# Rows of attention stored unscaled beside their norms; weight conversion from head pair 1

## The chip, the cores and the metric

One core of one Trainium2 chip runs the whole program in one launch. The metric is device time in microseconds (us). A core has a matrix engine (PE, with its weight loads PEld), a vector engine (DVE), an activation engine (ACT), GpSimd (POOL) and a sync engine (SP); each runs its own instructions in order, and they meet through semaphores. Here SP and POOL issue the DMAs: SP the plain loads, POOL the indirect ones and the stores of x.

## The reference, cut to what matters

```
kv  = k^T v per batch and head           # 8 x 8 heads, 576 x 64
o   = q kv ; x = o / rms(o) * g_norm     # rms over the 64 columns of a head
logits = x @ w_gate                      # 4608 tokens, 8 experts
# greedy assignment in order of falling logits, 576 tokens for each expert
for e in experts: y[mask_e] = relu(x[mask_e] @ w1[e]) @ w2[e]
h = y @ w_in ; out = (h * cos(h)) @ w_out
```

x has 4608 rows of 512 columns (8 heads of 64). Each head of each row has one norm factor, 1/rms; g_norm is folded into w1 and w_gate.

## The kernel before

**Attention.** Batches go two at a time (four stages s), heads two at a time, so 16 head pairs n. For each, PE builds k^T v, transposes q and multiplies; ACT copies the result into `xs` (stage 1 uses the room of `wout`) and squares it, DVE sums the squares into `SS` and copies q and k^T v to SBUF. At the end of a stage `norm(s)` queues small steps on DVE that give the factors `R`; then POOL multiplies x by R in place, head pair by head pair (`scaled`, four instructions a stage), and stores the stage's 2304 KB to `x_rows` in HBM. The gate's logits are scaled by DVE with the same factors.

**Routing.** `Router.phase(k)` finds expert k's tokens: DVE compares keys, PE counts, eight rounds. Phase 0 stands between attention and the rest; phases 1 to 7 are worked in among later matmuls. `widx` (which weights) is known some us before `idx` (which tokens).

**Experts.** Tokens go in 16 blocks of 288 (`u`). `h`, `y`, `h2`, `outs` are the matmul stages of a block. POOL gathers the rows of x by `idx`, five tiles of up to 128 rows for an expert; `xtile` transposes a tile on PE, and ACT and DVE copy it out as two f16 halves. w1 and w2 of an expert are gathered by POOL; each is squared for a scale and split into a high half (ACT) and a low half (DVE).

**Conversion of the dense weights.** w_in and w_out come as 32 units of 512 KB in 64-bit words (`dense`). A unit is loaded by SP into one of three `io` buffers, scaled by ACT (`dG`) and merged by three DVE instructions into `stA` or `stB`. Four units make a block: two sums of squares on ACT, then for each of two tiles a high half on ACT and a low half on DVE (`win`, `wout`). All of w_in has to be done before `h2` of block 0, all of w_out (`("out", 3)`) before the first `outs`.

**What sets the order.** A planner (`Meter`, `Sched`) keeps a modelled clock for each engine while the program is written out. Pieces of the conversion are put between other work where they end no later than the modelled PE clock plus a slack (`PA` in attention). `GRANT` says after which head pair how many more units may be loaded. In attention the conversion starts after pair 4 (`n > 4`). `Sched.FILL` is the order in which kinds of fill are tried. `first_load` issues w1 and w2 of expert 0: all of w1 and the first two tiles of w2 as soon as `widx` is known, the other two once the second w1 tile is split and the gather of x is issued.

Of the kernel before, what the change touches and what calls it, by code (L numbers as in the profile page):

```python
# [8 lines left out]
F32 = mybir.dt.float32  # L9
# [4 lines left out]
OP = mybir.AluOpType  # L14
# [2 lines left out]

B, H, S, D = 8, 8, 576, 64
N, DM = B * S, H * D
E = 8  # L20
NCOL = 36


def dview(t, off, ap):
    return bass.AP(tensor=t.tensor, offset=t.offset + off, ap=ap)


PA = (3.6, 3.5, 33.0, 2.48, 2)
RB = 9
LOADED = 13  # L30
GRANT = {5: 1, 7: 1, 9: 1, 11: 1, 12: 2, 13: 99}
NHP = H // 2


def attention(nc, tc, q, k, v, w_gate, xrows, ident, gcol, L, M, sc):


    with ExitStack() as st:
# [27 lines left out]
        W2 = 2 * (D + E)  # L66
        KV = [one.tile([128, 2, NHP, W2], F32, name=f"KV{i}") for i in range(2)]
        SS = one.tile([128, NCOL, H], F32, name="SS")
        R = one.tile([128, NCOL, H], F32, name="R")
        kvt, qTs, XS, LR = {}, {}, {}, {}  # L70
        late, held = [], []
        M.prf = lambda: ps.tile([128, 4, 128], F32, name="pT", bufs=2).rearrange("p a b -> p (a b)")
# [73 lines left out]
        def o_mm(n, g):  # L146
            s, hp = divmod(n, NHP)
            if hp == 0 and g == 0:
                if s == 1:
                    XS[s] = M.wout2.rearrange("p i f d -> p (i f d)").bitcast(F32)[:, 0:RB * H * D].rearrange(  # L150
                        "p (r h e) -> p r h e", r=RB, h=H)
                else:
                    XS[s] = wk.tile([128, RB, H, D], F32, name="xs", bufs=2)
                LR[s] = wk.tile([128, RB, H, E], F32, name="LR", bufs=2)
            qT, kv = qTs.pop((n, g)), kv_of(n)
            pO = ps.tile([128, 2, 512], F32, name="pO", bufs=2)
            J, N = (1, 1) if g == 2 else (2, 2)
            for j in range(J):
                for a in range(2):
                    o = (D + E) * (2 * j + a)  # L160
                    for X in range(2):
                        for i in range(N):
                            h = slice(64 * i, 64 * i + 64)
                            nc.tensor.matmul(pO[64 * X:64 * X + 64, i, o:o + D + E],
                                             qT[h, 2 * j + X, 64 * a:64 * a + 64],
                                             kv[h, X, (D + E) * a:(D + E) * a + D + E], start=True, stop=True)
            hs = slice(2 * hp, 2 * hp + 2)
            if g < 2:
                po = pO[:, :, 0:2 * W2].rearrange("p i (j e) -> p j i e", j=2)
                rows = lambda x: x[:, 4 * g:4 * g + 4, hs].rearrange("p (j i) a e -> p j i (a e)", i=2)  # L170
                srows = lambda x: x[:, 4 * g:4 * g + 4, hs]
                lrows = lambda x: x[:, 4 * g:4 * g + 4, hs].rearrange("p (j i) a e -> p j i a e", i=2)
            else:
                po = pO[:, 0, 0:W2]
                rows = lambda x: x[:, 8, hs].rearrange("p a e -> p (a e)")
                srows = lrows = lambda x: x[:, 8, hs]
            sq = wk.tile([128, 4, 2, D], F32, name="sq", bufs=2)
            sqv = sq[:, 0].rearrange("p a e -> p (a e)") if g == 2 else sq.rearrange("p (j i) a e -> p j i (a e)", i=2)
            nc.scalar.activation(sqv, po[..., E:E + 2 * D], AF.Square)
            nc.scalar.activation(rows(XS[s]), po[..., E:E + 2 * D], AF.Copy)  # L180
            later()
            nc.vector.tensor_copy(lrows(LR[s]), gates(po))
            nc.vector.tensor_reduce(srows(SS[:, RB * s:RB * s + RB]), sq[:, 0] if g == 2 else sq, axis=AX, op=OP.add)
            later()
            if g == 2 and hp == NHP - 1:
                norm(s)

        def norm(s):
            c = slice(RB * s, RB * s + RB)
            a, y, w = (wk.tile([128, RB, H], F32, name=nm, bufs=1) for nm in ("na", "ny", "nw"))  # L190
            x = XS[s]
            m = LR[s]

            def scaled(i):
                h = slice(2 * i, 2 * i + 2)
                nc.gpsimd.tensor_mul(x[:, :, h], x[:, :, h], R[:, c, h, None].to_broadcast([128, RB, 2, D]))

            def store():
                nc.gpsimd.dma_start(dview(xrows, 2 * s * S * DM, [[RB * DM, 128], [1, RB * DM]]),
                                    x.rearrange("p r h e -> p (r h e)"))  # L200

            def stored():
                if s in HOLD:
                    held.append(store)
                else:
                    store()

            late.extend([
                lambda: nc.vector.tensor_scalar(a, SS[:, c], 1.0 / D, 1e-6, op0=OP.mult, op1=OP.add),
                lambda: nc.scalar.activation(w, a, AF.Sqrt),  # L210
                lambda: nc.vector.reciprocal(y, w),
                lambda: nc.vector.scalar_tensor_tensor(w, y, -0.5, y, op0=OP.mult, op1=OP.mult),
                lambda: nc.vector.tensor_mul(w, w, a),
                lambda: nc.vector.scalar_tensor_tensor(R[:, c], w, 1.5, y, op0=OP.add, op1=OP.mult),
                lambda: nc.vector.tensor_mul(m, m, R[:, c, :, None].to_broadcast([128, RB, H, E])),
                lambda: nc.vector.tensor_reduce(L[:, c, :], m.rearrange("p r h e -> p r e h"), axis=AX, op=OP.add),
            ] + [lambda i=i: scaled(i) for i in range(NHP)] + [stored])

        def side():
            later()  # L220
# [5 lines left out]
        for n in range(NP + 1):  # L226
            steps = []
            if n < NP:
                steps.append(lambda: kv_mm(n))
            if n:  # L230
                steps += [lambda: (o_mm(n - 1, 0), tr(n - 1, 2))]
            if n < NP:
                steps.append(lambda: kw_t(n))
            if n:
                steps.append(lambda: o_mm(n - 1, 1))
            if n < NP:
                steps.append(lambda: (tr(n, 0), kw_mm(n)))
            if n:
                steps.append(lambda: o_mm(n - 1, 2))
            if n < NP:  # L240
                steps.append(lambda: tr(n, 1))
            M.grant += GRANT.get(n, 0)
            for f in steps:
                f()
                if n == LOADED:
                    while held:
                        held.pop(0)()
                    HOLD.clear()
                if n > 4:
                    side()  # L250
                else:
                    later()
# [458 lines left out]
class Sched:  # L711
# [3 lines left out]

    FIRST = ("w0", "x0")
    FILL = ("w0", "x0", "l0", "bt", "bd", "bg", "p")

    def __init__(self, meter):
        self.m = meter
# [153 lines left out]
class Moe:  # L876
# [252 lines left out]
    def first_load(self, which, room, alloc):  # L1129
        sc, js = self.sc, (range(2), range(2, 4))  # L1130
        while 0 not in self.R.widx:
            yield WAIT
        for i in range(2):
            if i:
                for mark in room:
                    yield from sc.until(mark)
            for j in js[i]:
                yield "gpsimd", 1.04, self.R.known
                self.load_w(which, 0, [j], alloc[i])
                self.land[which, j] = self.nc.last  # L1140
# [42 lines left out]
    def gather(self, k, js=range(5)):  # L1183
        cb = 9 * k // 2
        for j in js:
            n = 64 if j == 4 and k % 2 == 0 else 128
            if k:
                t = self.pers.tile([128, 1024], F32, name="io", bufs=3)[:, 0:DM]
            else:
                t = self.tmp.tile([128, 2, U], F32, name=("et", "et", "eg", "eg", "ek")[j], bufs=1 + (j < 4))  # L1190
                t = t.rearrange("p a b -> p (a b)")[:, 0:DM]
            self.nc.gpsimd.indirect_dma_start(
                out=t[0:n], out_offset=None, in_=self.xrows,
                in_offset=bass.IndirectOffsetOnAxis(ap=self.R.idx[0:n, cb + j:cb + j + 1], axis=0))
            self.xg[k, j] = t, self.nc.last

    def xtrans(self, k, js=range(5), pre={}):
        for j in js:
            if j in pre:
                self.gather(k, [pre[j]])  # L1200
            yield from self.sc.after(self.xg[k, j][1])
            self.xtile(k, j)
            yield "both"

    def first_x(self, js):
        for j in js:
            yield "tensor", 0.45, self.xg[0, j][1]
            self.xtile(0, j)

    def xtile(self, k, j):  # L1210
        nc = self.nc
        r0, r1 = (64, 128) if k % 2 and j == 0 else (0, 64) if k % 2 == 0 and j == 4 else (0, 128)
        n = r1 - r0
        pos = 128 * j - 64 * (k % 2 and j > 0)
        x = self.xg[k, j][0]
# [203 lines left out]

def body(ctx, tc, q, k, v, g_norm, w_gate, w1, w2, w_in, w_out, out):  # L1420
    nc = Meter(tc.nc)
    xrows = nc.dram_tensor("x_rows", (N, DM), F32, kind="Internal").ap()
    ctx.enter_context(tc.manual_schedule())
    pers = ctx.enter_context(tc.tile_pool(name="pers", bufs=1))
    sm = ctx.enter_context(tc.tile_pool(name="sm", bufs=2))
# [49 lines left out]
    M.far = True  # L1475
    for n in range(E):
        sc.add("route", R.phase(n), ("route", n))
    sc.add("l0", M.first_load(1, (), [istage, istage]))
    sc.add("l0", M.first_load(2, (("w1", 0, 1), "gx"), [istage, istage]))
    sc.add("w0", M.first_w(1), ("w1", 0))  # L1480
    sc.add("w0", M.first_w(2), ("w2", 0))
    GP = (0.39, 1.67, 38.72, 0.83)
# [105 lines left out]
```

## Time and profile before

| | us |
|---|---|
| median of 3 runs (1458.42 to 1464.58) | 1463.87 |
| the profiled execution | 1462.46 |
| its span, first to last instruction | 1460.7 |
| PE / DVE / ACT / POOL busy in the span | 1334.3 / 890.4 / 617.8 / 190.7 |
| attention; routing phase 0 (to `idx`) | 0 to 150; 150 to 195 |
| first blocks, w_out conversion ends the wait | 195 to 323 |

The profiled execution lies 1.41 us under the median. The page's forty slices show PE at 9 tenths or more from the tenth slice on, and at 2 to 8 in the nine before. Nearly every compute instruction is recorded at one helper's line (L689), so instructions are told apart by the tiles that they write and read.

### The profile page before, as it was taken

To read this page: it belongs to the slowest core of one execution; us is meant where nothing else is said; L and a number is where in the kernel's file an instruction comes from. 1 tells how busy PE (TensorE), PEld (TensorE's weight loads), DVE (VectorE), ACT (ScalarE), POOL (GpSimd) and SP (SyncE) were. 2 spreads that over 40 slices of the span, in tenths; PEclk is the share of its full clock that TensorE was granted. 3 is DMA by queue.
4 is the path that set the end of the run, shared out by engine and by line. 5 is a ranking of instruction groups with operands and counts; after the bars stand their busy time and mean duration, and the time that the engine had idled before them with its cause. 6 is when DMAs were issued, how large, how long until landed. Compare 5 with 4: busy or idle time off the path is not lost.

```text
span 1460.7 us, 28545 instructions
## 1 busy us (share of the span) xinstructions
PE 1334.3 (91%) x12072; PEld 910.9 (62%) x12072; DVE 890.4 (61%) x2096; ACT 617.8 (42%) x1031; POOL 190.7 (13%) x211
## 2 busy tenths in 40 slices
PE   5877248859999999999999999999999999999997
PEld 4656235636667574666667675867676667676663
DVE  2658888887858676586667673655365426544350
ACT  2546255744625341446134621653256225533240
POOL 0222240003011111022002100130022001000000
PEclk8886559979999999999999999999999999999999
DMA  7795353213111111032002200140013002000000
GB/s 276 268 340 226 123 180 113 70 62 123 51 66 42 65 31 65 9 95 73 1 16 91 73 2 22 34 133 2 15 60 104 1 22 71 18 1 15 8 8 22
DMA packets 40367, 109.32 MB, mean 75 GB/s; under 512 B 4272, under 2 KB 12464, under 8 KB 39728
## 3 DMA queue, kind: packets, MB, share of 16 engines
q0 software_dynamic: 15744, 62.40, 12.5%
q1 hardware_dynamic: 23808, 45.09, 8.9%
q8 instruction: 94, 1.54, 0.4%
q14 instruction: 33, 0.27, 0.1%
q10 hardware_dynamic: 688, 0.02, 0.0%
HBM read 88.62 MB, written 18.87 MB: 74 GB/s over the span
## 4 chain that ended last, share of the span: by engine, by line
PE 77%; DVE 4%; ACT 2%; DMA 1%; issue 1%; POOL 0%; POOLq 0%; ACTq 0%; DVEq 0%; SPq 0%
PE ph L689 74%; PE pr L689 3%; PE pq L689 1%; DVE eg L689 1%; DVE stB L689 0%; ACT junk L689 0%; DMA sti<-in_moe_w_dram,wi 0%; DVE yT L689 0%; DMA io<-in_moe_w_out_dram 0%; DMA stB<-in_moe_w_dram,wi 0%; ACT ek L689 0%; DVE gT L689 0%; DVE stA L689 0%; ACT wout L689 0%; DVE wout L689 0%
## 5 line engine op out<-in xcount | busy, mean ns | idle before, releaser
L689 PE MATMUL ph<-wout,gT 128*128 128x512 f16 x1728 | 390.2, 380 | 5.0 <-DVE eg L689 2.6
L689 PE MATMUL ph<-yT,win 128*128 128x288 f16 x3072 | 384.2, 286 | 0.9 <-DVE eg L689 0.8
L689 PEld LDWEIGHTS <-win 128*128 128x128 f16 x3072 | 297.6, 98 | 78.9 <-DVE eg L689 1.8
L689 PEld LDWEIGHTS <-gT 128*128 128x128 f16 x1728 | 162.6, 98 | 202.4 <-ACT junk L689 11.1
L689 ACT ACTIVATE ek<-ph,quarter,us 128x576 int32<-128x576 f32 x128 | 106.3, 830 | 327.1 <-PE ph L689 320.1
L689 PE MATMUL ph<-xT,w1s 128*128 128x288 f16 x1536 | 202.7, 291 | 9.3 <-DVE hT L689 6.4
L689 PE MATMUL ph<-hT,w2s 128*128 128x288 f16 x1536 | 202.7, 286 | 0.0
L689 DVE SCALAR_TENSOR_TENSOR et<-ph,us,ek 128x576 f32<-128x576 f32 x128 | 104.6, 817 | 135.5 <-ACT ek L689 135.2
L689 PEld LDWEIGHTS <-w1s 128*128 128x128 f16 x1536 | 149.5, 99 | 50.8 <-DVE hT L689 3.7
L689 PEld LDWEIGHTS <-w2s 128*128 128x128 f16 x1536 | 146.2, 98 | 36.3
L689 POOL DMA_INDIRECT out_dram<-eg,idx x36 | 36.7, 1021 | 606.6 <-DVE scT L689 299.5
L689 DVE SCALAR_TENSOR_TENSOR eg<-ph,cG,et 128x576 f32<-128x576 f32 x128 | 103.5, 809 | 2.7 <-ACT et L689 1.3
L689 DVE TENSOR_TENSOR gT<-eg,gT 128x576 f16<-128x576 f32 (+2 forms) x192 | 99.6, 550 | 0.7
L689 ACT ACTIVATE gT<-eg 128x576 f16<-128x576 f32 (+2 forms) x192 | 92.3, 513 | 14.9 <-DVE eg L689 14.9
L689 ACT ACTIVATE et<-et,qtr 128x576 f32<-128x576 f32 x128 | 97.9, 765 | 0.6 <-DVE et L689 0.6
L689 DVE TENSOR_TENSOR eg<-ph,scT 128x512 f32<-128x512 f32 x36 | 24.9, 692 | 112.9 <-PE ph L689 109.0
L689 ACT ACTIVATE yT<-ph,sy 128x576 f16<-128x576 f32 x32 | 22.0, 737 | 163.1 <-DVE sy L689 156.8
L689 DVE SCALAR_TENSOR_TENSOR hT<-ph,hT 128x576 f16<-128x576 f32 x64 | 48.0, 755 | 50.0 <-ACT hT L689 49.7
L689 ACT ACTIVATE hT<-ph 128x576 f16<-128x576 f32 x64 | 40.9, 646 | 82.4 <-PE ph L689 82.4
L689 POOL DMA_INDIRECT io<-x_rows,idx x35 | 34.2, 978 | 240.7 <-PE pq L689 198.5
L689 POOL DMA_INDIRECT stA<-in_moe_w_dram,wi x28 | 29.8, 1063 | 225.0 <-issue 187.8
L689 PE MATMUL pO<-KV,qTs 64*64 64x72 f32 x1152 | 41.0, 264 | 12.5 <-issue 9.9
(209 smaller groups left out, 1328.7 us busy)
## 6 DMA issues: line engine op xcount, KB each, us to landing
kt<-in_k_dram SPq DMA_DIRECT2D x16, 576.0 KB, 5.2
vt<-in_v_dram SPq DMA_DIRECT2D x16, 576.0 KB, 6.6
qt<-in_q_dram SPq DMA_DIRECT2D x16, 576.0 KB, 7.4
io<-in_moe_w_in_dram SPq DMA_DIRECT2D x16, 512.0 KB, 6.6
io<-in_moe_w_out_dram SPq DMA_DIRECT2D x16, 512.0 KB, 3.5
x_rows<-xs POOLq DMA_DIRECT2D x3, 2304.0 KB
x_rows<-wout POOLq DMA_DIRECT2D x1, 2304.0 KB
out_dram<-eg,idx POOLq DMA_INDIRECT x36
```

The lines of the kernel that those rows point to most:

```text
L689: return f(*a, **kw)
```

## The change

`R` is gone. A row of x is now 520 values: 512 unscaled columns and the 8 factors, written by DVE into the last 8 columns of `xs`; rows of `x_rows` are 2080 bytes. POOL's sixteen multiplications are gone, and the stage's store is queued right behind the logits. The factor is applied after the gather: `xnorm`, one DVE instruction a tile (40 tiles, five an expert), ahead of the tile's transposes. Conversion may be placed from head pair 1 on, one unit granted for each pair, with other slacks. w2's first two tiles are loaded after the gather of x. x is tried before w0 in `FILL` and `FIRST`.

```diff
-PA = (3.6, 3.5, 33.0, 2.48, 2)
+PA = (2, 2, 33.0, 2.48, 2)
-GRANT = {5: 1, 7: 1, 9: 1, 11: 1, 12: 2, 13: 99}
+GRANT = {**dict.fromkeys(range(1, 13), 1), 13: 99}
...
-            def scaled(i):
-                h = slice(2 * i, 2 * i + 2)
-                nc.gpsimd.tensor_mul(x[:, :, h], x[:, :, h], R[:, c, h, None].to_broadcast([128, RB, 2, D]))
...
-                lambda: nc.vector.scalar_tensor_tensor(R[:, c], w, 1.5, y, op0=OP.add, op1=OP.mult),
+                lambda: nc.vector.scalar_tensor_tensor(r, w, 1.5, y, op0=OP.add, op1=OP.mult),
...
-            ] + [lambda i=i: scaled(i) for i in range(NHP)] + [stored])
+                stored,
+            ])
...
-                if n > 4:
+                if n:
                     side()
...
-    FIRST = ("w0", "x0")
-    FILL = ("w0", "x0", "l0", "bt", "bd", "bg", "p")
+    FIRST = ("x0", "w0")
+    FILL = ("x0", "w0", "l0", "bt", "bd", "bg", "p")
...
     def xtrans(self, k, js=range(5), pre={}):
-        for j in js:
+        for j in (*js, None):
+            if j is not None:
+                yield from self.sc.after(self.xg[k, j][1])
+                self.xnorm(k, j)
+            if j != js[0]:
+                self.xtile(k, js[-1] if j is None else j - 1)
...
+    def xnorm(self, k, j):
+        r0, r1 = self.xspan(k, j)
+        x = self.xg[k, j][0][r0:r1]
+        y = x[:, 0:DM].rearrange("p (h e) -> p h e", h=H)
+        self.nc.vector.tensor_mul(y, y, x[:, DM:XW, None].to_broadcast([r1 - r0, H, D]))
...
-    sc.add("l0", M.first_load(1, (), [istage, istage]))
-    sc.add("l0", M.first_load(2, (("w1", 0, 1), "gx"), [istage, istage]))
+    sc.add("l0", M.first_load(1, ((), ()), [istage, istage]))
+    sc.add("l0", M.first_load(2, (("gx",), (("w1", 0, 1),)), [istage, istage]))
```

On POOL, at the end of attention and the gather for expert 0 (`sti` are the tiles of w1 and then w2; `et`, `eg`, `ek` the tiles of x), before:

```order
L689 TENSOR_TENSOR xs<-xs,R 128x9x128 x4
L689 DMA x_rows<-xs 128x4608
L689 DMA sti<-in_moe_w_dram,wi 128x1024 x6
L689 DMA et<-x_rows,idx 128x512 x2
L689 DMA eg<-x_rows,idx 128x512 x2
L689 DMA ek<-x_rows,idx 64x512
L689 DMA sti<-in_moe_w_dram,wi 128x1024 x2
```

The same place on POOL now:

```order
L687 DMA x_rows<-wout 128x4680
L687 DMA x_rows<-xs 128x4680 x2
L687 DMA sti<-in_moe_w_dram,wi 128x1024 x4
L687 DMA et<-x_rows,idx 128x520 x2
L687 DMA eg<-x_rows,idx 128x520 x2
L687 DMA ek<-x_rows,idx 64x520
L687 DMA sti<-in_moe_w_dram,wi 128x1024 x4
```

The multiplications are gone, and two tiles of w2 stand behind the gather instead of ahead of it.

On DVE, where expert 0's x is turned into `xT` and w1 is split (`peb` to `sg` is w1's scale), before:

```order
L689 TENSOR_SCALAR peb<-pq 128x1
L689 TENSOR_SCALAR s_3020<-peb 128x1
L689 TENSOR_TENSOR sg<-s_3020,gcol 128x1
L689 TENSOR_SCALAR stB<-dG 128x512
L689 SCALAR_TENSOR_TENSOR stB<-dG,stB 128x512
L689 TENSOR_TENSOR xT_2429<-ph,xT_2428 128x4x128 x3
L689 TENSOR_TENSOR xT_2429<-pq,xT_2428 128x4x128
L689 TENSOR_TENSOR xT_2429<-pq,xT_2428 128x4x64
L689 SCALAR_TENSOR_TENSOR w1s_2425<-sti,sg,w1s_2424 128x1024
```

The same place on DVE now:

```order
L687 TENSOR_SCALAR peb<-pq 128x1
L687 TENSOR_SCALAR s_3066<-peb 128x1
L687 TENSOR_TENSOR sg<-s_3066,gcol 128x1
L687 TENSOR_TENSOR et<-et 128x512
L687 SCALAR_TENSOR_TENSOR w1s_2456<-sti,sg,w1s_2455 128x1024
L687 TENSOR_TENSOR et<-et 128x512
L687 TENSOR_TENSOR xT_2460<-ph,xT_2459 128x4x128
L687 TENSOR_TENSOR eg<-eg 128x512
L687 TENSOR_TENSOR xT_2460<-ph,xT_2459 128x4x128 x2
L687 TENSOR_TENSOR eg<-eg 128x512
L687 SCALAR_TENSOR_TENSOR w1s_2456<-sti,sg,w1s_2455 128x1024
```

The factors' multiplications (`et<-et`, `eg<-eg`) stand between, the first low half of w1 comes ahead of the transposed tiles, and the merges have left this place.

On DVE, behind the last product (`eg`) of block 0's `h2`, before:

```order
L689 TENSOR_TENSOR gT_3313<-eg,gT_3312 128x2x288 x2
L689 TENSOR_SCALAR g_4109<-pr 15x8
L689 SCALAR_TENSOR_TENSOR stA<-io,stA 128x512
L689 TENSOR_SCALAR stA<-dG 128x512
L689 SCALAR_TENSOR_TENSOR stA<-dG,stA 128x512
L689 SCALAR_TENSOR_TENSOR stA<-io,stA 128x512
L689 TENSOR_REDUCE amy<-ph 128x1
```

The same place on DVE now:

```order
L687 TENSOR_TENSOR gT_3346<-eg,gT_3345 128x2x288 x2
L687 SCALAR_TENSOR_TENSOR stB<-dG,stB 128x512
L687 TENSOR_REDUCE nS<-pr 128x1
L687 TENSOR_TENSOR base<-base,nS 128x1
L687 SCALAR_TENSOR_TENSOR cmp<-hi,base,i_73 128x540
L687 TENSOR_REDUCE amy<-ph 128x1
L687 SCALAR_TENSOR_TENSOR stB<-io,stB 128x512
```

Of the 32 merges, 25 stood ahead of this place and 29 do now; of w_out's eight low halves two stood ahead of it and four do now. Ahead of routing phase 0 stood 7 merges and 2 low halves of w_in, and now 11 and 4; by the time that phase 0 has written `idx` it was 11 and 2, and is now 16 and 4.

## Rows read from the trace of the kernel before

**Rows 1.** Busy time by stage; the columns stand in its first line.

```profile
core 0: us, PE busy (x) PEld busy (x) DVE busy (x) ACT busy (x) POOL busy (x), PEclk, DMA share, GB/s
0.00:150.00 150.00, 107.59 (x2721) 86.93 (x2721) 87.15 (x230) 74.96 (x188) 31.15 (x30) 0.82 0.76 274
150.00:195.00 45.00, 12.07 (x336) 10.55 (x337) 38.69 (x108) 9.01 (x15) 16.61 (x11) 0.51 0.40 138
195.00:305.00 110.00, 88.52 (x696) 64.28 (x696) 94.19 (x197) 70.29 (x104) 9.43 (x7) 0.89 0.34 111
305.00:321.00 16.00, 0.45 (x3) 0.31 (x3) 12.82 (x29) 9.57 (x15) 0.00 (x0) 0.59 0.19 64
321.00:1460.70 1139.70, 1125.65 (x8317) 748.79 (x8315) 657.54 (x1535) 453.93 (x714) 133.53 (x163) 1.00 0.13 43
```

**Rows 2.** Timeline of PE: start, us, instruction, idle before and releaser.

```profile
319.10 0.16 PE L689 MATMUL pq<-psb,ones 128*128 128x1 bf16 x1 [10.83 <-DVE psb L689]
```

**Rows 3.** Timeline of DVE at the start of phase 0, then of phase 1.

```profile
151.55 0.76 DVE L689 TENSOR_TENSOR LR<-LR,R 128x576 f32<-128x576 f32 x1
...
154.53 2.10 DVE L689 TENSOR_SCALAR key<-m 128x36 int32<-128x36 int32 x1
...
156.92 2.11 DVE L689 TENSOR_TENSOR key<-key,m 128x36 int32<-128x36 int32 x1
...
159.32 1.79 DVE L689 TENSOR_SCALAR ti<-key 128x36 int32<-128x36 int32 x1
...
210.48 0.21 DVE L689 TENSOR_SCALAR key<-m 128x36 int32<-128x36 int32 x1
```

**Rows 4.** Timeline of DVE late in attention, beside POOL's multiplications.

```profile
90.87 2.62 DVE L689 SCALAR_TENSOR_TENSOR stA<-io,stA 128x512 int32<-128x512 int32 x1
...
124.49 1.88 DVE L689 TENSOR_SCALAR stB<-dG 128x512 int32<-128x512 int32 x1
...
126.57 2.34 DVE L689 SCALAR_TENSOR_TENSOR stB<-dG,stB 128x512 int32<-128x512 int32 x1
...
129.43 2.01 DVE L689 SCALAR_TENSOR_TENSOR stB<-io,stB 128x512 int32<-128x512 int32 x1
```

**Rows 5.** Timeline of PE in attention, where it waits for DVE.

```profile
94.52 0.51 PE L689 MATMUL pT<-ident,KV 64*64 64x64 f32 x6 [2.44 <-DVE qTs L689]
...
131.82 0.37 PE L689 MATMUL pT<-ident,KV 64*64 64x64 f32 x2 [1.83 <-DVE KV L689]
```

**Rows 6.** Groups of DVE from 195 to 323: busy, mean ns, idle.

```profile
L689 DVE SCALAR_TENSOR_TENSOR stB<-dG,stB 128x512 int32<-128x512 int32 x12 | 8.3, 690 | 0.3
L689 DVE SCALAR_TENSOR_TENSOR stB<-io,stB 128x512 int32<-128x512 int32 x12 | 8.2, 685 | 0.1
...
L689 DVE SCALAR_TENSOR_TENSOR stA<-io,stA 128x512 int32<-128x512 int32 x9 | 6.2, 688 | 0.2
...
L689 DVE SCALAR_TENSOR_TENSOR win<-stB,s,win 128x1024 f16<-128x1024 f32 x4 | 5.1, 1276 | 0.0
...
L689 DVE TENSOR_SCALAR stB<-dG 128x512 int32<-128x512 int32 x12 | 5.0, 419 | 0.0
```

**Rows 7.** Timeline of POOL around expert 0's gather.

```profile
151.66 9.40 POOL L689 TENSOR_TENSOR xs<-xs,R 128x1152 f32<-128x1152 f32 x4 [19.89 <-ACT dG L689]
...
195.17 1.33 POOL L689 DMA_INDIRECT et<-x_rows,idx  x1 [0.30 <-issue]
...
199.31 1.92 POOL L689 DMA_INDIRECT eg<-x_rows,idx  x1 [0.30 <-issue]
...
213.58 2.23 POOL L689 DMA_INDIRECT sti<-in_moe_w_dram,wi  x1 [2.16 <-DVE w1s L689]
```

**Rows 8.** Timeline of PE in `h` of block 0.

```profile
209.76 8.71 PE L689 MATMUL ph<-xT,w1s 128*128 128x288 f16 x46 [1.78 <-DVE w1s L689]
...
225.78 1.49 PE L689 MATMUL ph<-xT,w1s 128*128 128x288 f16 x6 [3.43 <-DVE hT L689]
```

**Rows 9.** Waits of PE from 321 on: total, times, longest.

```profile
PE ph L689 <- DVE eg L689: 3.7, 4, 1.9
```

More of the change, by code (lines that the diff above doesn't have):

```diff
@@ L19 @@
 N, DM = B * S, H * D
+XW = DM + H
 E = 8
@@ L68, in attention @@
         SS = one.tile([128, NCOL, H], F32, name="SS")
-        R = one.tile([128, NCOL, H], F32, name="R")
         kvt, qTs, XS, LR = {}, {}, {}, {}
@@ L149, in o_mm @@
                 if s == 1:
-                    XS[s] = M.wout2.rearrange("p i f d -> p (i f d)").bitcast(F32)[:, 0:RB * H * D].rearrange(
-                        "p (r h e) -> p r h e", r=RB, h=H)
+                    XS[s] = M.wout2.rearrange("p i f d -> p (i f d)").bitcast(F32)[:, 0:RB * XW].rearrange(
+                        "p (r c) -> p r c", r=RB)
                 else:
-                    XS[s] = wk.tile([128, RB, H, D], F32, name="xs", bufs=2)
+                    XS[s] = wk.tile([128, RB, XW], F32, name="xs", bufs=2)
                 LR[s] = wk.tile([128, RB, H, E], F32, name="LR", bufs=2)
@@ L166, in o_mm @@
                                              kv[h, X, (D + E) * a:(D + E) * a + D + E], start=True, stop=True)
-            hs = slice(2 * hp, 2 * hp + 2)
+            hs, cs = slice(2 * hp, 2 * hp + 2), slice(2 * D * hp, 2 * D * hp + 2 * D)
             if g < 2:
                 po = pO[:, :, 0:2 * W2].rearrange("p i (j e) -> p j i e", j=2)
-                rows = lambda x: x[:, 4 * g:4 * g + 4, hs].rearrange("p (j i) a e -> p j i (a e)", i=2)
+                rows = lambda x: x[:, 4 * g:4 * g + 4, cs].rearrange("p (j i) c -> p j i c", i=2)
                 srows = lambda x: x[:, 4 * g:4 * g + 4, hs]
@@ L174, in o_mm @@
                 po = pO[:, 0, 0:W2]
-                rows = lambda x: x[:, 8, hs].rearrange("p a e -> p (a e)")
+                rows = lambda x: x[:, 8, cs]
                 srows = lrows = lambda x: x[:, 8, hs]
@@ L192, in norm @@
             m = LR[s]
-            def scaled(i):
-                h = slice(2 * i, 2 * i + 2)
-                nc.gpsimd.tensor_mul(x[:, :, h], x[:, :, h], R[:, c, h, None].to_broadcast([128, RB, 2, D]))
+            r = x[:, :, DM:XW]
             def store():
-                nc.gpsimd.dma_start(dview(xrows, 2 * s * S * DM, [[RB * DM, 128], [1, RB * DM]]),
-                                    x.rearrange("p r h e -> p (r h e)"))
+                nc.gpsimd.dma_start(dview(xrows, 2 * s * S * XW, [[RB * XW, 128], [1, RB * XW]]),
+                                    x.rearrange("p r c -> p (r c)"))
             def stored():
@@ L213, in norm @@
                 lambda: nc.vector.tensor_mul(w, w, a),
-                lambda: nc.vector.scalar_tensor_tensor(R[:, c], w, 1.5, y, op0=OP.add, op1=OP.mult),
-                lambda: nc.vector.tensor_mul(m, m, R[:, c, :, None].to_broadcast([128, RB, H, E])),
+                lambda: nc.vector.scalar_tensor_tensor(r, w, 1.5, y, op0=OP.add, op1=OP.mult),
+                lambda: nc.vector.tensor_mul(m, m, r[..., None].to_broadcast([128, RB, H, E])),
                 lambda: nc.vector.tensor_reduce(L[:, c, :], m.rearrange("p r h e -> p r e h"), axis=AX, op=OP.add),
-            ] + [lambda i=i: scaled(i) for i in range(NHP)] + [stored])
+                stored,
+            ])
         def side():
@@ L1133, in first_load @@
         for i in range(2):
-            if i:
-                for mark in room:
-                    yield from sc.until(mark)
+            for mark in room[i]:
+                yield from sc.until(mark)
             for j in js[i]:
@@ L1187, in gather @@
             if k:
-                t = self.pers.tile([128, 1024], F32, name="io", bufs=3)[:, 0:DM]
+                t = self.pers.tile([128, 1024], F32, name="io", bufs=3)[:, 0:XW]
             else:
                 t = self.tmp.tile([128, 2, U], F32, name=("et", "et", "eg", "eg", "ek")[j], bufs=1 + (j < 4))
-                t = t.rearrange("p a b -> p (a b)")[:, 0:DM]
+                t = t.rearrange("p a b -> p (a b)")[:, 0:XW]
             self.nc.gpsimd.indirect_dma_start(
@@ L1197, in xtrans, with xspan @@
     def xtrans(self, k, js=range(5), pre={}):
-        for j in js:
+        for j in (*js, None):
[4 more added lines that the diff above has]
+                self.xtile(k, js[-1] if j is None else j - 1)
             if j in pre:
                 self.gather(k, [pre[j]])
-            yield from self.sc.after(self.xg[k, j][1])
-            self.xtile(k, j)
-            yield "both"
+            if j is not None:
+                yield "both"
     def first_x(self, js):
-        for j in js:
-            yield "tensor", 0.45, self.xg[0, j][1]
-            self.xtile(0, j)
+        normed = {}
+        for j in (*js, None):
+            if j is not None:
+                yield "vector", 0.68, self.xg[0, j][1]
+                self.xnorm(0, j)
+                normed[j] = self.nc.last
+            for i in [i for i in normed if i != j]:
+                yield "tensor", 0.45, normed.pop(i)
+                self.xtile(0, i)
+    def xspan(self, k, j):
+        return (64, 128) if k % 2 and j == 0 else (0, 64) if k % 2 == 0 and j == 4 else (0, 128)
+    def xnorm(self, k, j):
[3 more added lines that the diff above has]
+        self.nc.vector.tensor_mul(y, y, x[:, DM:XW, None].to_broadcast([r1 - r0, H, D]))
     def xtile(self, k, j):
         nc = self.nc
-        r0, r1 = (64, 128) if k % 2 and j == 0 else (0, 64) if k % 2 == 0 and j == 4 else (0, 128)
+        r0, r1 = self.xspan(k, j)
         n = r1 - r0
@@ L1421, in body @@
     nc = Meter(tc.nc)
-    xrows = nc.dram_tensor("x_rows", (N, DM), F32, kind="Internal").ap()
+    xrows = nc.dram_tensor("x_rows", (N, XW), F32, kind="Internal").ap()
     ctx.enter_context(tc.manual_schedule())
```

## The prediction

> **What bounds the kernel now.** I read the busy time by stage first, because one share over the whole span mixes stages with different limits. From 321 us on PE is busy 1125.65 of 1139.7 us at the full granted clock [rows 1]: that stage is bound by PE, and nothing that frees another engine can shorten it by more than its 14 us. All that can be won lies ahead of 321, in four pieces. Attention (0 to 150) is mixed: PE 72%, DVE 58%, the DMA engines 76%. Routing phase 0 (150 to 195) is a chain of short DVE and PE steps at half the clock: DVE is busy 38.69 of 45 us. From 195 to 305 DVE is busy 94.19 of 110 us, more by share than PE (88.52). From 305 to 321 PE does nothing (0.45 us) while DVE is busy 12.82 of 16. The timeline of PE says for whom it waits there: for `psb`, the scale of the last block of w_out [rows 2]. So the first `outs` waits for the conversion of the dense weights, and behind that conversion stands DVE. The groups of DVE in that stretch are to be read next [rows 6]: 12 and 9 merges ended there and the low halves of w_in are still among them. So between 195 and 323 one microsecond of DVE is worth close to one microsecond of the whole.
>
> The other thing to see is that some DVE instructions are far longer than their like. At the start of phase 0 three instructions on 36 columns take 2.10, 2.11 and 1.79 us, and the first of them takes 0.21 in phase 1 [rows 3]. In just that time POOL runs its four multiplications of the last stage, 151.66 to 161.06, 2.35 us each [rows 7]. The same is seen late in attention: 2.62, 1.88, 2.34 and 2.01 us [rows 4] for forms whose mean is 0.69, 0.42, 0.69 and 0.69 [rows 6].
>
> **The change part by part.**
>
> *POOL's multiplications go: phase 0.* The three held instructions come to 6.00 us; at 0.21 each they are 0.63. They follow each other on the chain that begins phase 0, where PE has nothing to do, so all of it counts: -5.4. The last store of x was issued behind the multiplications, long before the gather at 195.17 [rows 7], so that it goes earlier is worth nothing.
>
> [...] POOL keeps all its indirect DMAs, one gather of `eg` took 1.92 us to issue where one of `et` took 1.33 [rows 7], and the new multiplications now stand on DVE just there. [...]
>
> *POOL's multiplications go: attention.* The four held instructions [rows 4] come to 8.85 us against 2.48 for their like. PE waited behind them 2.44 and 1.83 us [rows 5], 4.3 together. I take -4.3.
>
> *Conversion moves into attention.* By the order on DVE, four merges and two low halves more stand ahead of phase 0. A merge is 0.419 + 0.690 + 0.685 = 1.79 us, a low half 1.276 [rows 6]: 4 x 1.79 + 2 x 1.276 = 9.7 us of DVE. DVE has 62.85 of 150 us free there [rows 1], but it runs in order, and a merge ahead of a copy that PE waits for is seen on PE, as rows 5 show. The ends are 0 (all in the gaps) and +9.7 (all seen); no row tells which, so I take the half, +4.9. ACT gains four scalings and one block's sums and high halves; it has 75 of 150 us free. The loads for it are 12 units by pair 12 instead of 6: six times 512 KB, 3.1 MB, at 274 GB/s 11.5 us of DMA time, in a stage whose DMA engines idle 24%, 36 us. They stand on SP's queue between loads of k, v and q that are issued three pairs ahead, so I take 0; the other end is +11.5. Attention together: +0.6, between -4.3 and +5.4 without the DMA.
>
> *Phase 0 holds five merges instead of four.* 1.8 us of DVE, in waits for PE's counts (6.3 us free on DVE there, rows 1). I take 0; end +1.8.
>
> *The stretch from 195 to 323.* Before, 21 merges end there (12 + 9, rows 6), and one of them had its first two steps behind it; now 16. That is 5 x 1.79 - 1.11 = 7.8 us less. Two low halves of w_in less: 2.6. Against it stand five norm multiplications of expert 0. The trace of before has none on POOL's data in SBUF for DVE; the nearest row multiplies 576 columns by the same kind of repeated factor in 0.76 [rows 3], so 512 columns are 0.68, and five are 3.4. Sum: -7.8 - 2.6 + 3.4 = -7.0. The order at block 0's last product says where this is seen: 7 merges and 6 low halves of w_out were still to come there (7 x 1.79 + 6 x 1.276 = 20 us), now 3 and 4 (10 us). So the wait of 16 us should shrink to 6 to 9. Since DVE is not busy without a gap (80 to 86%), half of -7.0 is one end. The other comes from w2: its tiles are loaded behind x now, but the last one, issued at 213.58 behind a wait for `w1s` [rows 7], can go sooner because the first low half of w1 comes sooner on DVE. What PE loses there is 3.43 us [rows 8], so the end is -7.0 - 3.4 = -10.4. x itself: its transposes now wait for a multiplication (+0.7), while PE's first long run waited for `w1s` on DVE until 209.76 anyway [rows 8]; I take 0.
>
> *The 35 tiles of the other experts.* 35 x 0.68 = 23.7 us more DVE from 321 on, where it is busy 58%. PE waited there 3.7 us in all for `eg` of DVE [rows 9]. Each multiplication is written a step ahead of its transposes, with other matmuls between. Ends 0 and +23.7; I take +1, near the lower end, because the row for PE's waits on DVE is so small. The rows of x are 2080 bytes instead of 2048, 1.6% of a transfer that is not waited for there: 0.
>
> Sum: -5.4 + 0.6 - 7.0 + 1.0 = -10.8. Against the profiled execution, 1462.46, that is 1451.7. That execution lies 1.4 under the median, 1463.87; I don't add that.
>
> **The rivals.**
>
> A, attention takes what it is given. The conversion placed there is seen one for one (+9.7 - 4.3 = +5.4), and in the stretch after it PE's own chain (`h`, `y`, `h2`) keeps half the gain (-3.5). For it speaks PE's waiting for DVE in rows 5 and that DVE's share there is already 58%; against it that DVE still has 63 us free there, six times what is added. -5.4 + 5.4 - 3.5 + 1 = -2.5: 1460.0.
>
> B, slower: the norm on the path of every later tile. PE runs in order, so a transpose that waits for its multiplication stops the matmuls behind it. If each of the 35 is seen in full, +23.7 instead of +1: -11.8 + 23.7 = +11.9, 1474.4. The point at which it decides: the other terms come to -11.8, and slower by 0.5% is 8.7 above the profiled execution, so each tile must cost (8.7 + 11.8) / 35 = 0.59 us. For it speaks that PE has no slack from 321 on; against it the 42% of DVE that is free and rows 9.
>
> C, the earlier loads are in the way. If k, v and q come later by the 11.5 us that the six units take: 1463.1. For it speaks the 76% of DMA in attention, the highest share of any stage; against it that loads are issued three pairs ahead.
>
> D, better than summed: early conversion fits wholly in gaps (-4.3), and w2's wait goes too (-10.4): -5.4 - 4.3 - 10.4 + 1 = -19.1: 1443.4.
>
> **How the numbers follow.** Forecast (1446 to 1457) 0.50, D 0.18, A 0.16, B 0.08, C 0.08. 0.5% of the median, 7.3 us, is about what a measurement of this kernel can tell from no change; faster is under 1456.5, slower over 1471.2. Faster: nearly all of the forecast, all of D, a fifth of A: 0.69. Slower: B and a rest: 0.09. Same: 0.22. The range takes in D and A and C's edge and leaves out B and the far tails: 1440 to 1463.
>
> **What would show it.** In the profile after: `key` and `ti` at the start of phase 0 at 0.2 us each, and phase 0 some 5 us shorter from `na` to `idx`; attention ending within 5 us of 150; 16 merges between `idx` and the last `wout`, and PE's empty stretch ahead of the first `outs` down from 16 to under 10 us; PE's share from there on still at 98% or more. Wrong it is if attention ends over 5 us later (A, C: look at waits of PE for `qTs` or for loads), if PE waits for the multiplications of `io` in later blocks (B), or if the empty stretch stays at 16 us although DVE has less to do there.

## The result, and the profile after

The kernel after takes 1445.81 us (median of 4 runs, 1441.56 to 1449.99), the kernel before 1463.34 in the same comparison: a ratio of 0.9886, 95% interval 0.9847 to 0.9925. Timed again beside other kernels it gave 1444.08 (6 runs), 0.9880 [0.9858, 0.9902]. Faster was forecast, with 1451.7 and a range of 1440 to 1463; the gain is 17.5 us where 10.8 were summed up.

The profiled execution of the kernel after spans 1442.2 us, 18.5 less than that of before. To see where, both spans are cut at the same three events: the last stage's `na` (the first step of its norm, the end of attention), the first write of `idx`, and the first `outs`. Windows of before, columns as in [rows 1]:

```profile
0.00:149.59 149.59, 107.59 (x2721) 86.93 (x2721) 86.95 (x230) 74.78 (x186) 31.15 (x30) 0.82 0.76 274
149.59:193.62 44.03, 12.07 (x336) 10.55 (x337) 37.65 (x100) 8.67 (x14) 15.67 (x10) 0.51 0.38 130
193.62:320.88 127.26, 88.85 (x698) 64.49 (x698) 108.13 (x233) 80.25 (x118) 10.37 (x8) 0.85 0.33 108
320.88:1460.70 1139.82, 1125.77 (x8317) 748.90 (x8316) 657.66 (x1535) 454.05 (x714) 133.53 (x163) 1.00 0.13 43
```

The same windows of after:

```profile
0.00:144.60 144.60, 103.92 (x2722) 83.43 (x2722) 88.72 (x248) 80.47 (x196) 3.29 (x18) 0.87 0.81 299
144.60:183.97 39.37, 12.08 (x337) 10.63 (x338) 33.77 (x109) 13.60 (x21) 5.27 (x5) 0.52 0.49 168
183.97:300.15 116.18, 87.67 (x701) 63.67 (x700) 99.85 (x212) 68.97 (x102) 9.72 (x9) 0.90 0.30 93
300.15:1442.20 1142.05, 1127.00 (x8313) 748.65 (x8312) 678.65 (x1569) 452.37 (x714) 147.07 (x163) 0.99 0.13 43
```

The first number behind a window is its length. Attention is 5.0 us shorter, phase 0 4.7, the stretch from `idx` to the first `outs` 11.1, and the rest 2.2 longer: -18.6, the 18.5 of the spans but for rounding. PE is still busy 98.7% of the rest.

The start of phase 0 on DVE in after, against [rows 3]:

```profile
149.43 0.18 DVE L687 TENSOR_SCALAR key<-m 128x36 int32<-128x36 int32 x1
...
149.92 0.19 DVE L687 TENSOR_TENSOR key<-key,m 128x36 int32<-128x36 int32 x1
...
150.41 0.17 DVE L687 TENSOR_SCALAR ti<-key 128x36 int32<-128x36 int32 x1
```

6.00 us have become 0.54. PE ahead of the first `outs` in after, against [rows 2] and the empty 16 us of before:

```profile
296.04 0.16 PE L687 MATMUL pq<-psb,ones 128*128 128x1 bf16 x1 [1.49 <-DVE g L687]
300.15 0.59 PE L687 MATMUL ph<-wout,gT 128*128 128x512 f16 x1 [3.95 <-ACT wout L687]
301.47 1.01 PE L687 MATMUL ph<-wout,gT 128*128 128x512 f16 x2 [0.74 <-DVE wout L687]
```

The wait of 10.83 for `psb` is gone; 1.49 + 3.95 are left, the chain of the last block's scale. Groups of DVE between `idx` and the last low half of w_out in after, against [rows 6]:

```profile
L687 DVE SCALAR_TENSOR_TENSOR stB<-io,stB 128x512 int32<-128x512 int32 x8 | 5.5, 689 | 0.2
...
L687 DVE SCALAR_TENSOR_TENSOR stA<-io,stA 128x512 int32<-128x512 int32 x8 | 5.5, 686 | 0.1
...
L687 DVE SCALAR_TENSOR_TENSOR win<-stA,s,win 128x1024 f16<-128x1024 f32 x2 | 2.5, 1274 | 0.0
...
L687 DVE TENSOR_TENSOR et<-et 128x512 f32<-128x512 f32 x2 | 1.4, 688 | 0.0
```

8 + 8 merges end there instead of 21, and a row's multiplication takes the 0.68 us that were estimated. PE's waits in attention, first before, then after (total, times, longest):

```profile
PE pT L689 <- DVE qTs L689: 11.6, 12, 2.4
...
PE pT L689 <- DVE KV L689: 4.2, 2, 2.4
```

```profile
PE pT L687 <- DVE qTs L687: 8.0, 13, 1.6
...
PE pT L687 <- DVE KV L687: 3.7, 4, 2.3
```

PE waits 4.1 us less for DVE's copies, but other waits grew: its idle time in attention fell by 1.3 us only, from 42.0 to 40.7. The other 3.7 us are busy time.

### The profile page after: what moved, and what is told of

Read it like the earlier page. It is cut to its first block, busy times and chain, and to the rows that moved or that the text cites. A ratio compares the mean times of both kernels' runs of the same rounds, so it can differ in the third digit from the quotient of the medians.

```text
span 1442.2 us, 28591 instructions
## 1 busy us (share of the span) xinstructions
PE 1330.7 (92%) x12072; PEld 906.4 (63%) x12072; DVE 901.0 (62%) x2136; ACT 615.4 (43%) x1031; POOL 165.3 (11%) x195
## 4 chain that ended last, share of the span: by engine, by line
PE 83%; DVE 9%; issue 3%; ACT 2%; DMA 2%; POOL 1%; ACTq 0%; POOLq 0%; DVEq 0%
PE ph L687 74%; PE pr L687 3%; PE pT L687 2%; PE P L687 1%; PE pO L687 1%; PE pq L687 1%; DVE stB L687 1%; DVE SS L687 1%; DMA wgr<-in_moe_w_gate_dram 1%; DVE stA L687 1%; DVE cmp L687 1%; DVE eg L687 1%; DVE qTs L687 1%; DVE w1s L687 1%; DVE wout L687 0%
## 5 line engine op out<-in xcount | busy, mean ns | idle before, releaser
L687 POOL DMA_INDIRECT io<-x_rows,idx x35 | 39.7, 1135 | 254.4 <-PE pq L687 202.4
L687 POOL DMA_INDIRECT stA<-in_moe_w_dram,wi x28 | 35.5, 1270 | 199.8 <-issue 193.1
```

Source lines behind the costliest of these rows:

```text
L687: return f(*a, **kw)
```

## The experiments

Theory T: POOL's multiplications hold DVE wherever the two overlap, and the conversion left behind `idx` holds PE; the change takes away both. The rivals are named in the expectations. Every kernel's profile was cut at the same three events (lengths in us, each of one profiled execution; median over all its runs, ratio to the kernel before timed beside it):

| kernel | to `na` | to `idx` | to `outs` | rest | median | ratio [95%] |
|---|---|---|---|---|---|---|
| before | 149.6 | 44.0 | 127.3 | 1139.8 | 1460 to 1463 | 1 |
| after | 144.6 | 39.4 | 116.2 | 1142.1 | 1445.8 | 0.9886 [0.9847, 0.9925] |
| f1 after, again | 143.6 | 39.4 | 117.0 | 1143.4 | 1444.1 | 0.9880 [0.9858, 0.9902] |
| e1 rows only | 144.7 | 39.4 | 127.6 | 1141.3 | 1450.8 | 0.9932 [0.9908, 0.9955] |
| e2 conversion only | 157.3 | 44.0 | 112.8 | 1137.5 | 1453.2 | 0.9947 [0.9929, 0.9964] |
| e3 after, late conversion | 141.5 | 39.4 | 132.1 | 1141.9 | 1457.2 | 0.9971 [0.9952, 0.9990] |
| e4 after, old loads and fill | 147.3 | 39.4 | 118.5 | 1147.7 | 1450.7 | 0.9922 [0.9891, 0.9952] |
| f2 after, POOL times one | 154.4 | 40.3 | 119.1 | 1143.9 | 1455.2 | 0.9964 [0.9947, 0.9982] |
| f3 after, no later norms | 147.0 | 39.4 | 116.9 | 1143.0 | 1446.6 | 0.9898 [0.9873, 0.9923] |
| f4 after, more units | 150.0 | 40.4 | 117.4 | 1137.3 | 1449.2 | 0.9925 [0.9902, 0.9947] |
| g1 after, old fill | 145.9 | 39.4 | 118.0 | 1148.4 | 1453.0 | 0.9940 [0.9919, 0.9962] |
| g2 after, old w2 loads | 142.2 | 40.6 | 115.1 | 1142.9 | 1445.0 | 0.9899 [0.9878, 0.9920] |
| g3 after, small norm of expert 0 | 146.7 | 39.4 | 117.4 | 1141.9 | 1447.4 | 0.9906 [0.9883, 0.9929] |
| h1 after, lows in phase 0 | 151.0 | 40.3 | 119.7 | 1143.3 | 1454.5 | 0.9947 [0.9929, 0.9966] |

One thing is to be read first. The kernels after, f1, e4, f3, g1, g2 and g3 run the same instructions in attention, and it lasts 142.2 to 147.3 us (median 145.9), PE busy 102.9 to 110.8 at a granted clock of 0.87 to 0.81. So a difference of 5 us between two single profiles says little there; medians over such groups say more. Of the kernel before there is one profile only.

**e1, the rows alone** (kernel before, with only the new rows and `xnorm`):

```diff
...
-            ] + [lambda i=i: scaled(i) for i in range(NHP)] + [stored])
+                stored,
+            ])
...
```

> The kernel before with only the rows changed: factors beside unscaled rows, no multiplication on POOL, one on DVE after each gather; conversion from head pair 5 and the order of loads as before. 12 merges by idx (before 11, after 16). Theory T (POOL's multiplications and the later conversion both cost time, and add up): attention ends 1 to 5 us earlier, `key` and `ti` give 5.4, five norms of expert 0 less one merge cost 1.6, later norms 2: about 1457, 4 to 8 under before; PE's wait ahead of the first `outs` stays at 14 to 18. Rival R1 (the whole gain is the conversion placed early; POOL's multiplications stood where nothing was lost): 1463 to 1468, since only the norms' cost is left. Rival R2 (the order of w2's and x's loads makes the gain): as R1, 1463 to 1468.

1450.8: faster than T said, and R1 and R2 fall. Phase 0 has the whole of its gain; attention is 4.9 shorter; the stretch to `outs` stays, and PE still waits for `psb` there:

```profile
309.95 0.16 PE L687 MATMUL pq<-psb,ones 128*128 128x1 bf16 x1 [9.04 <-DVE psb L687]
```

**e2, the conversion alone** (kernel before):

```diff
-PA = (3.6, 3.5, 33.0, 2.48, 2)
+PA = (2, 2, 33.0, 2.48, 2)
-GRANT = {5: 1, 7: 1, 9: 1, 11: 1, 12: 2, 13: 99}
+GRANT = {**dict.fromkeys(range(1, 13), 1), 13: 99}
...
-                if n > 4:
+                if n:
```

> The kernel before with only the conversion placed from head pair 1 (grants and slacks of the kernel after); POOL still multiplies and rows are stored scaled. 11 merges ahead of phase 0 and 15 by idx instead of 7 and 11. Theory T: four merges and two low halves less behind idx, 9.8 us, of which 7 to 10 are seen; more merges meet POOL's multiplications, so attention ends 0 to 5 us later than before; 1453 to 1460, and `key`, `ti` stay at about 2 us. R1: 1443 to 1447, all of the gain and more, with no norms to pay. R2: 1461 to 1465.

1453.2, within T, though both of its parts are larger than expected: the stretch to `outs` gains 14.4 and attention loses 7.7. Why it loses, the timeline of DVE shows, beside POOL's four multiplications of one stage (92.75 to 102.27):

```profile
95.38 2.63 DVE L689 SCALAR_TENSOR_TENSOR stB<-io,stB 128x512 int32<-128x512 int32 x1
...
100.31 2.50 DVE L689 SCALAR_TENSOR_TENSOR stB<-dG,stB 128x512 int32<-128x512 int32 x1
```

These take 0.69 when POOL is quiet. More merges in attention meet POOL more often: the 33 merge steps of e2's attention take 32.2 us on DVE, and the same steps in the kernel after 19.7. Before, 21 steps take 19.8 us, where 12.6 would be their time beside a quiet POOL (seven merges of 1.79).

**e3, the kernel after with the late conversion** (e2's diff the other way):

> The kernel after with the conversion again from head pair 5 (grants and slacks of the kernel before). Theory T: the first kernel of this call plus the load order, 1453 to 1457; PE's wait ahead of the first `outs` back at 13 to 17 us. R1: 1461 to 1466, the gain gone. R2: 1446 to 1450, most of the gain kept.

1457.2, at T's upper end; 11 to 13 us of the gain go with the early conversion, and PE waits for `psb` again ahead of `outs`, 3.25 and 10.82 us. Against e1 it differs only in loads and fill and is slower by 6: the stretch to `outs` is 132.1 with DVE busy 110.3, in e1 127.6 with 110.0. DVE stands idle 4 us longer there; why was not settled.

**e4, the kernel after with the order of loads and fill of before:**

```diff
-    FIRST = ("x0", "w0")
+    FIRST = ("w0", "x0")
...
-    sc.add("l0", M.first_load(2, (("gx",), (("w1", 0, 1),)), [istage, istage]))
+    sc.add("l0", M.first_load(2, (("w1", 0, 1), "gx"), [istage, istage]))
```

> The kernel after with w2's first two tiles loaded ahead of the gather of x again, and w0 tried before x0. Theory T: 1445 to 1449, within 3 us of the kernel after, since DVE's load up to the first `outs` is the same. R1: the same. R2: 1454 to 1460, most of the gain gone.

1450.7, 5 to 7 over the kernel after: neither T nor R2. Up to `outs` it is the kernel after within what single profiles tell; the rest is 5.6 longer. g1 and g2 take it apart. With e1, e2 and e4 the two large parts can be set beside each other: the rows alone gain 10, the conversion alone 8, both 11 with the old order and 17 with the new one (ratios times 1462).

**f1, the kernel after again:**

> The kernel after, unchanged, beside the others of this call. 1442 to 1450. In its profile: `na` at 141 to 147, `na` to `idx` 39.4, `idx` to the first `outs` 114 to 119, the rest 1141 to 1143.

As expected, but for the last window (1143.4 against 1143).

**f2, POOL's multiplications put back, by ones:**

```diff
...
+                nc.gpsimd.tensor_mul(z, z, un[:, :, 2 * i:2 * i + 2, None].to_broadcast([128, RB, 2, D]))
...
```

> The kernel after with POOL's sixteen multiplications put back at their old place, on the same data, but by ones, and the stores again behind them; rows, norms, conversion and loads stay those of the kernel after. Theory T (POOL's arithmetic itself holds DVE, and the more the more merges are in attention): `key`, `ti` back at about 2 us each, `na` to `idx` 43 to 45 instead of 39.4; PE idle in attention up from 40.7 to 47 to 51, attention 6 to 13 us longer; behind `idx` nothing; 1456 to 1464, 11 to 18 over the kernel after. Rival R3 (the gain of the new rows is that the steps at a stage's end are fewer and the stores earlier, and DVE's long instructions are a by-product that costs nothing): at most 3 over the kernel after.

11.1 over f1; R3 falls. The expectation was wrong on one point: ones are there from the start, so POOL multiplies as soon as ACT has written a head pair, all ahead of `key`, and phase 0 is hardly touched. Most of the price is in attention: 10.8 of the 14.3 us between the two profiled executions. Nor is it a price of later stores: each stage's store is still issued 0.8 us behind DVE's factors, as in the kernel after. PE is idle 46.1 us in attention (154.36 - 108.26), 38.8 in f1. Groups of DVE in attention, f1 and then f2:

```profile
L687 DVE COPY qTs<-pT 128x512 f32<-128x512 f32 x16 | 11.0, 687 | 1.3 <-PE pT L687 1.3
...
L687 DVE SCALAR_TENSOR_TENSOR stB<-io,stB 128x512 int32<-128x512 int32 x4 | 2.7, 684 | 0.0
L687 DVE TENSOR_SCALAR stB<-dG 128x512 int32<-128x512 int32 x4 | 1.7, 425 | 0.1
...
L687 DVE TENSOR_SCALAR na<-SS 128x72 f32<-128x72 f32 x3 | 0.6, 199 | 0.1
```

```profile
L692 DVE COPY qTs<-pT 128x512 f32<-128x512 f32 x16 | 10.9, 683 | 1.3 <-PE pT L692 1.3
L692 DVE SCALAR_TENSOR_TENSOR stB<-io,stB 128x512 int32<-128x512 int32 x4 | 5.6, 1400 | 0.0
L692 DVE TENSOR_SCALAR na<-SS 128x72 f32<-128x72 f32 x3 | 5.4, 1793 | 0.1
L692 DVE TENSOR_SCALAR stB<-dG 128x512 int32<-128x512 int32 x4 | 4.2, 1056 | 0.0
```

DVE is busy 104.97 us in f2's attention and 88.92 in f1's, 16 more, nearly all of it in merges (11.3) and `na` (4.8); the copies out of PSUM stay as short as ever.

**f3, no multiplication of the later experts' rows:**

```diff
                 yield from self.sc.after(self.xg[k, j][1])
-                self.xnorm(k, j)
```

> The kernel after without the multiplication of the gathered rows for experts 1 to 7: their x stays unscaled, 35 DVE instructions and 23.9 us of DVE less; expert 0's five stay. Theory T (they are hidden beside PE, a step ahead of the transposes): 0 to 3 us under the kernel after, and PE's waits from the first `outs` on down by at most 3. Rival B of the prediction (each is on the path): 20 to 24 under.

Not faster at all. The stretch behind the first `outs`, f1 and then f3:

```profile
299.96:1443.40 1143.44, 1127.60 (x8313) 748.92 (x8312) 678.51 (x1569) 453.45 (x714) 147.28 (x163) 0.99 0.13 43
```

```profile
303.31:1446.30 1142.99, 1127.83 (x8313) 749.14 (x8312) 658.79 (x1534) 452.54 (x714) 144.62 (x163) 0.99 0.13 43
```

DVE does 19.7 us less and the stretch is 0.45 shorter, less than the 1.4 us by which f1 and the kernel after differ there. The later norms are hidden; rival B falls.

**f4, more conversion in attention:**

```diff
-GRANT = {**dict.fromkeys(range(1, 13), 1), 13: 99}
+GRANT = {**dict.fromkeys(range(1, 13), 1), 1: 2, 4: 2, 8: 2, 12: 2, 13: 99}
```

> The kernel after with a second unit granted after head pairs 1, 4, 8 and 12: 14 merges ahead of phase 0 instead of 11, and 19 merges and 6 low halves of w_in by idx instead of 16 and 4, 7.9 us of DVE moved ahead of idx. Theory T (behind idx DVE is the bound until PE's wait of 5.6 us ahead of the first `outs` is gone; a merge in attention costs a third of its time now that POOL is quiet): attention 1 to 3 us longer, idx to the first `outs` 4 to 7 shorter; 1440 to 1445, 1 to 5 under the kernel after. Rival R4 (attention has no more room, or its loads of k, v and q come late with DMA already busy 81%): attention 5 to 9 longer, 1447 to 1453.

R4 is right, for the first of its two reasons: 5 over f1, and no wait of PE for k, v or q but the first. Attention is 6.4 longer than in f1, phase 0 one, the stretch to `outs` not shorter, although DVE has 5.4 less to do in it. PE no longer waits ahead of `outs` there, and the conversion's waits have moved into attention: PE waits 4.1 us for `psb`, 2.0 for `kvt` and 2.0 for `xs`, where f1 has 0.4 for `kvt` and none of note for the others.

**g1 and g2, the order of fills and of w2's loads apart** (e4's diff, its first lines and its last):

> The kernel after with w0 tried before x0 again (`FILL`, `FIRST`); w2's first tiles still behind x. On DVE all four low halves of w1 (5.1 us) then stand between the first and the second multiplication of expert 0's rows. Theory F (of the order of loads and fills it is x before w0 that counts, because the rows' multiplications stand on DVE behind w1's halves): PE waits 4 to 5 us for the second `et`, the granted clock stays at half until 20 to 25 us behind idx instead of 15; 3 to 7 over the kernel after, 1448 to 1452. Rival G (it is w2's loads behind x): within 2 of the kernel after.

> The kernel after with w2's first two tiles loaded ahead of the gather of x again; x0 tried before w0. DVE's order is that of the kernel after. Theory F: within 2 of the kernel after, 1443 to 1447; x lands up to 2 us later behind two more indirect loads on POOL's queue. Rival G: 3 to 7 over the kernel after.

g1 is 7 to 9 over the kernel after, beyond F's 3 to 7, and g2 equal to it: it is x before w0. But Theory F had the place wrong. PE does wait 5.04 for the second `et`, and yet `idx` to `outs` is only 1 to 2 longer. Most of the price comes 80 us later, in `y` of expert 1's first block. POOL's load of expert 1's first w2 tile, and PE, in g1:

```profile
367.74 0.95 POOL L687 DMA_INDIRECT stA<-in_moe_w_dram,wi  x1 [0.30 <-issue]
```

```profile
383.77 0.16 PE L687 MATMUL pq<-psb,ones 128*128 128x1 bf16 x1 [5.34 <-DVE psb L687]
385.55 0.66 PE L687 MATMUL ph<-hT,w2s 128*128 128x288 f16 x2 [1.62 <-ACT w2s L687]
386.87 2.58 PE L687 MATMUL ph<-hT,w2s 128*128 128x288 f16 x10 [0.66 <-DVE w2s L687]
```

The same load of expert 1's first w2 tile in the kernel after:

```profile
335.23 0.94 POOL L687 DMA_INDIRECT stA<-in_moe_w_dram,wi  x1 [0.30 <-ACT xT L687]
```

With the old fill the planner comes to that load 32 us later, and PE waits 7.6 us for w2. e4 has the same three waits (5.34, 1.62, 0.66). e1, with the old fill and the late conversion, has none of them, so the price belongs to the two together; with the late conversion it is the new order that is slower (e3 against e1).

**g3, expert 0's multiplications cut to an eighth:**

```diff
-        y = x[:, 0:DM].rearrange("p (h e) -> p h e", h=H)
+        a = H if k else 1
+        y = x[:, 0:D * a].rearrange("p (h e) -> p h e", h=a)
...
```

> The kernel after with expert 0's five multiplications cut to the first of eight heads (64 columns of 512), so that seven heads of its rows stay unscaled; the order of the first ones on DVE stays. 5 x 0.5 = 2.5 us of DVE less, all behind idx and ahead of the first `outs`. If that stretch is bound by DVE throughout: 2 to 3 under the kernel after. If only where PE waits for a row's multiplication: PE's waits for `et` and `eg` (4.5 us together in the kernel after) shrink by 1 to 2, and 0 to 2 under the kernel after.

No gain: `idx` to `outs` is 117.4 with DVE busy 97.16 instead of 99.85. PE's first three waits for `et` and `eg` are 1.70, 1.41 and 0.97 against 2.17, 1.40 and 0.97. So the first reading of the expectation falls: 2.7 us of DVE are not 2.7 us of that stretch any more. Behind the first ones the planner's order differs from that of the kernel after, so no more than that is read from it.

**h1, less slack in attention:**

```diff
-PA = (2, 2, 33.0, 2.48, 2)
+PA = (1, 1, 33.0, 2.48, 2)
```

> The kernel after with the slacks of DVE and ACT in attention cut from 2 to 1 us: still 11 merges ahead of phase 0 and 16 by idx, but two of the four low halves of w_in (2.6 us of DVE) move from attention into phase 0, where PE waits anyway. If a piece in attention is seen on PE by a third of its time and phase 0 hides its own: 1 us under the kernel after, 1441 to 1446. If phase 0 is full (DVE was busy 33.8 of its 39.4 us): phase 0 longer by 1 to 2.6, 1444 to 1448.

Both wrong: 9 to 10 over the kernel after. Attention takes 151.0 although it does less conversion, since the pieces stand elsewhere; PE's waits for ACT's `qTs` are 6.2 us there and 1.7 in the kernel after. How much is put into attention says less than between which copies. No kernel tried beats the one after; g2 equals it.

## Why the prediction came out as it did

- **Phase 0: -5.4 forecast, -4.7 measured** in the kernel after; 44.0 us came down to between 39.4 and 40.6 in every kernel in which POOL is quiet in that chain. The three held instructions give 5.46. The rest went to a chain that now falls into phase 0, the scales of w_in's blocks: `psm`, `psb` and `peb` stand on DVE between `wi` and `tb`, which begin 1.23 us apart instead of 0.49. The merges themselves cost nothing there (e1 has six, after five, both 39.4).
- **Attention: +0.6 forecast, -5.0 measured. This is the term that was mis-sized most.** It was the sum of two. POOL's share, -4.3, came from two waits of PE [rows 5]; e1 and e3, which have only this part of the change there and one merge less, give -4.9 and -8.1. The conversion's share, half of 9.7 us, was the bare middle of 0 and 9.7; with POOL quiet it is roughly 2.8 (145.9, the median of seven, against 143.1, the mean of e1 and e3, which lie 3.2 apart). And the two are not independent, as the sum took them: with POOL at work the same conversion costs 7.7 (e2 against before, one profile each), and POOL lengthens DVE's merges in attention by 7.3 us before and by 12.5 in e2. Against the median of the seven the term is -3.7 (149.6 to 145.9). PE's waits for DVE's copies did fall by about what the forecast had from rows 5, but PE's idle time fell by 1.3 only, and its busy time for as many matmuls is 3.7 shorter at a granted clock of 0.87 instead of 0.82. How much of that clock is the change's can't be told, since it spans 0.81 to 0.87 over executions of the same instructions.
- **`idx` to the first `outs`: -7.0 forecast, -11.1 measured** (-10.2 in f1), about the end of -10.4, of which 3.4 was to come from w2. That reading of [rows 8] was wrong: the 3.43 us are a wait for DVE's `hT` and not for w2, and PE waits 3.52 there in the kernel after. DVE's busy time there fell by 8.3 (7.0 forecast), and 2.8 more came from DVE's idle time, which the forecast left as it was. That DVE bounds the stretch is shown by e1 and e3, where the wait for `psb` stays, and by e2, where it is gone; that it stops doing so once about 16 merges are done by `idx`, by f4.
- **Later norms: +1 forecast, 0.45 by f3.** The 2.2 us that the last window is longer are not theirs, since f3 has them too. f4 and e2 have 1137 there. In both the granted clock of the window is 1.00, and the products that open it take 0.81 us for three in f4, as later ones do (0.82 at 330.00 in before), and 0.38 for one in e2; in before and after the first one alone takes 0.59. Over the window's first 40 us the clock is 0.95 before and 0.92 in the kernel after. And f4 does 12 matmuls fewer behind the cut than f1. So what happens ahead of `outs` moves a few us from one side of the cut to the other.
- **w2's loads: 0 forecast, 0 measured** (g2). **x: 0 forecast**, and that was luck of the order: with the fill of before it would have been 7 to 9 (g1), at a place that the prediction didn't look at.
- **The rivals.** B (norms on the path) and C (loads in the way: DMA share 0.81 in attention, no wait of PE for k, v or q but the first) did not happen, nor did A. D, early conversion wholly in gaps and the stretch at its end, comes nearest with 1443.4 (1445.8 lies just outside the forecast's own 1446 to 1457): not because conversion is free in attention, but because POOL's share was larger than PE's two waits. Its other reason, w2's wait, had no part.
- **What POOL lengthens on DVE.** The long instructions of [rows 3] and [rows 4] were put down to POOL because they fall in the time of its multiplications; f2, which puts the multiplications back, shows it: against f1 `na` goes from 0.20 to 1.79 us and a merge step (`stB<-io,stB`) from 0.68 to 1.40 in the mean, while copies out of PSUM (`qTs`) stay at 0.68 and 0.69.
- **The issue of the gathers: 0 in the sum, and no loss seen.** In the kernel after, with the new multiplications on DVE, the five gathers of expert 0 take 0.95, 0.95, 0.95, 1.45 and 0.91 us to issue, 5.2 in all against 6.2 before; the longest is 1.45 against 1.92.

## What to carry to other kernels

Arithmetic on GpSimd beside a busy DVE is to be charged by what DVE does at that moment: here 16 multiplications, 35.4 us of POOL in f2, put 16 us on DVE and 11 on the whole. Removing such a disturbance and moving work into the place it leaves belong together: in attention the two gave -4.9 (e1) and +7.7 us (e2) one at a time, and -3.7 to -5.0 together. (On the whole time they nearly add, 10 and 8 against 17, but with the old order of loads and fill the two gave 11.) And an edit of order costed at nothing should be followed one load further than the stage that it is made for.

## What the runs showed of the hardware

Beside POOL's multiplications a DVE instruction can be far longer than its like: `key` on 36 columns took 2.10 us before and 0.18 in the kernel after, a merge step up to 2.64 in e2 where its like beside a quiet POOL takes 0.69. Others were not lengthened at all: in f2 and e2 every sum of squares (`SS<-sq`, 128x512) took 0.66 to 0.69 us and every copy out of PSUM (`qTs`, 128x512) 0.67 to 0.69, also where it lay wholly within a POOL multiplication (in f2 a sum at 99.62 and a copy at 116.55). And in all four stages before, `LR<-LR,R` started 0.1 us ahead of POOL's first multiplication and took 0.76, as long as its like beside a quiet POOL, while that multiplication took 2.6 us where the shortest takes 2.12. Second, the same instructions in attention ran 142 to 147 us from one execution to the next, with PE's granted clock at 0.81 to 0.87 there. That spread was not expected of a stage whose work is fixed, and it sets what a single profile can show.
